# A new stored order and engine choice for the 4,008 steps of an attention and gated MLP kernel

## The chip, the cores and the metric

One core of one Trainium2 chip. The metric is device microseconds (us) of one execution, the median of three runs. PE is TensorE, DVE VectorE, ACT ScalarE, POOL GpSimd, SP the queue that issues the transfers.

## The reference

Eight batches, eight heads, 576 positions, 64 columns a head. Attention has a bias that depends on the two positions through a small MLP; its output goes through a gated block.

```python
scores = scale * np.matmul(q, k.transpose(0, 1, 3, 2))
x = (psi_rel / psi_i)[..., None]
bias = np.maximum(x @ w1 + b1, 0.0) @ w2
scores = scores + bias.transpose(2, 0, 1)[None, :, :, :]
attn = softmax(scores)
x = (attn @ v).transpose(0, 2, 1, 3).reshape(B, S, H * D)
gate = sigmoid(causal_conv_5_taps(x, conv_w))
out = (gate * (x @ w_val)) @ w_out
```

## The kernel before

The program is first written as a list of steps. `Plan.add` takes for each step the engines that may do it, with a booked duration for each in us, a function that issues it, and the steps that it depends on. Nothing is issued then. `Plan.order` reads a stored table, `ORDER`: two bytes for each of the 4,008 steps, which give the step's number and which of its engines does it. The steps are issued in that order, so each engine's queue is the table's order cut to that engine, and buffers are handed out in the table's order as well. The booked durations and due times are not read when the kernel is built; the table was found with them elsewhere.

```python
for lo, hi in zip(code[:n], code[n:]):
    t = self.tasks[(lo + 256 * hi) // 4]
    t.on, t.done = t.engines[lo % 4], True
```

The stages are these.

The bias: 36 groups of 16 rows (`bias_rows`). Four `relu` steps of a group write the hidden values: the first on ACT (L329), the others on DVE or POOL (L331). `bias_mm` multiplies on PE (L350). `bias_fin` evicts on ACT (L369) or DVE (L371). `bias_store` writes to DRAM and `load_bias` reads skewed rows back.

The weights: `weight` decodes eight blocks of 64-bit numbers on DVE with six `double_step` steps each (L432 to L456), and splits each into two f16 parts (`w_hi`, `w_sub`, `w_lo`). All six steps are booked alike:

```python
[("V", 0.38 * n / 512 + 0.05)]
```

Attention: 32 steps of `pair`, each for two heads of a batch and four or five blocks of 128 queries. For each block PE multiplies (`qkm` L712, `qkr` L728), DVE adds the bias and finds the maximum (`logits` L758), ACT takes the exponential (`expo` L770). In 24 of the pairs the result is split in two f16 parts: `top` copies (L209 on ACT, L211 on DVE, L213 on POOL), `rest` and `rest8` subtract (L232 on DVE or POOL, 1,024 and 128 columns), and `swap` transposes by a transfer (L935). In eight pairs `norm` scales (L820 on POOL, L227 on ACT) and `tp` transposes on PE (L901). `piece` (L970) multiplies by the values, `vlo` (L667) being the low part of these.

The gated block (`mlp`), one for each batch: the convolution (`taps` L1163), `split_hi` and `split_lo` (L220 on DVE), `val` (L1231), the gate (`gf` L1241), `ghi` (L209, L211 or L213) and `glo` (L232), then `outp` (L1297), `ote` and the store. `ghi` and `glo` of the wider part issue two instructions, of 256 and of 64 columns. Between two `qkm` of a pair the table places steps of other pairs and of the gated blocks.

Of the kernel before, what the change touches and what calls it, by code (L numbers as in the profile page):

```python
# [51 lines left out]
    'w*booAkxY-'
    'XeN2%FTPAD?#qA>@nus`XLJ%c67gHvWr#5?maB@w@MVh2Ym)oPEB!{!e*z7nR3OBv2c9+H6l3cFHrMklLFStCNR@>L}_6MC>+8+p38mY|}cSe7o$tH98ZtoAnL@4P?O&b~whS%WYWvaDoemp6q#Yi-'
    'kXg6{-_YX43(@wTouPD_*FPHy?RK+TG4@oidz}6pnOC#UdUvp0AuFF3Num`-'
    'yJ*{{hfney>psn5rHHWQmJL=bbuTT`qRZ(i<f$%7zlxmoL+#;@IrTl3{wmpeEG~HUTSI0?PM0v+yciJ3SBMSG?#668fL$MEV!V`(cmG60d{lpKP$#9CI)1hiuRP32tzEJnO0>x6y&IH+yn{H<-'
    'Ta2`$-ht#uM5D1uwEDwZy*&K3oNA<}nbDY=#*=(i5Ph!ZN3E9vqjoUs_XKm*dNUO6bn~5r*Eb#vC#hbs)$PAK?e#O+DK;A8lW9Ri<Vel?7zXzZZuCDb=VOg_pc5=4Xre+EsbZ-Vs?-`8I-'
    '9G15$AA%q-'
    'dtg?3DASNirNM^fk>2UTrBh{=fJi327|SuoA=AU^KQnvYEsr?sSQ(k}S8WPHtbaISR=ib(OqEPG@@kQkl*&fuOy}@q^*$PlCh=whMv`$zkIo=ZntYimqnMW^Z@u4lmzrxZSj~Y4>@et<tEFdok8?d*'
    'Gz}uO);2VZK~^Gw${<DaT}*c#UOwu^oB$uQ@n(sTv6TJpH`i8tiAFO1C!7Mri+_pz-'
    '?3{@$<xmvuV%GCanLWT~2C;3lEy2CJ!Y3?}pOj}ijgUf|{!UQ}$&q~LJcU8!^@bDnJlf>`9ESH5cG3V0Nkrm3_P3YT+k4-'  # L60
    'xg{<%E)q#cg(nE0b8wbn{OrAzI2hH)EBmyHw_gpV$1gdZTA57Gt$iDx1#bo2_Ig60i6Al}dXQFSMJjPCL=X`_;xc-fWfp0SiIH1q>$6`-'
    'AMTnqfN0R4>;b42z>lI@=|SW2)!Ok<@gW@BC2X8IIWebX3q_99%7zcRbM-'
    'O66|F>#MNky4)D2CW_5%ceGtx8vjt=CEFGrgOX#<?|V<J6U;l+;I^7D{M^?k?2i6ZW+*y+ZdMp^BAM~Hsj=igmSlfG42Iw$_ydzE9*u<qK`C-'
    ';Q#2S+BnKlZPSb3H6NAol=4m!3J%$xjl95nk$P1}yGy#u7!Z92r!{chKmX<Y>@46_vyWSZ2YV2D))AT5u&HnY9@La?*DZ=0B_TE;!fw6|f7(Cr_IbP4Ou{V`!jiR|MJTK1XSH+UGO4NCwEw?1uUMSP'
    'WQaP2V#FLd;Sow>7!&YmyewucO)oFc@^ZM#RpC4mjBeFaG%0()9{AGW@A9(Y*$V<`Kw?bh@BpL{YBTiR59t?TI?<7O9Ml_Lbw&LwhERjj}+%G3nzHG{=abb8dPQ<+3KAEiitXiwnWp^r9alx|ERKCD'
    'uvZZ>Xna<??xmQd$^ZnvrSnU>4#dN*Ve!n+#Hwvv%CRFKoYVF^BHi74>U+PS2@Jb3tvakh|yXE*lCYXIs+1q<{Fu>RmJ{l+c;|~eA8k9sAYITNXxm=1DL|LjRnXHp96ec;2ce!oEq*2sx)5mtKlWw}'
    ')okru8rlUFfWm&2C{2tg{@#+{Vb?~0|4+E^*Yfh$UZ&q663i+DN9%<WNcYHXkcSrpJzerG_55payM-rmc>yL*1vEY;cICx0c2F}3HHy%FcmjmNz)b6MSnF&0LEa!A#SP-'
    '`Lsh9DEj)k!C@0=;kcQqP!gp0=L1Wxz^n`!$fS8oL~<WKVss9mU24ZM+xCy5+G!>hAMGFUpB<MMo?*;1rD`*xLLGcR!-UiL)gnBs^hgo{UQo88$-'
    'rc*X&+v|JI@0v^{Z>(hRmMc}e`<2YgzNE|VdovVxIhD@D6O!<^o&X<gcf3hQ&>bjx!fYfO_H}#xfj^ke#57pwlW-'
    '&^WFt{A_F6ocionGb<B8C3>xp=w_@i_(Q%ZNrl}xEz%VrmH^`TTLSG*m$HwyP7)o5}+Wk37ZW~<xk4RT#vp_$>A1Z^$a?4{wj|Ge{YVOkhZMq|xXgOL;5?jQ(~aj_Kp*zIvn+CjoCbFLik<rG^g6is'  # L70
    'C9j>iRzFOpO)Uo61`*Q4vwG*&8~@01%JZ#WYF`L8PNYSYJd$aj+dK)Ld;PNmZHfU9*it>1qx!#+|Axp<)|W36UJ`Jmq$j{2j#*s|@|+XI3eGsEWw3j#5L_25o;-#-'
    '7s7<PL5WH_3RCmpF$m1MS9a@6WilouP*LPJASIDN=7!Elr1I&F=hV7$%V5i1PK6-'
    '8^w_JRxVw%U<sg1{UvyTd#gWravgjKeEC(HkZE#!w92eq&869Bn>~BwJ!^GT0oqJ3scOGqlT%O>rWgNJ@bq$?z;Eh&H<s&O7L1rIe@YkZYXi9|FPa^riSbQ%}E@RRo*#K!FX~?FwWZj$kfigJ-efaX'
    'UTVX@;DxmNy)RyMb=UqOot|9j`Bxc|8=*y3-k-J)6tsB5~3mpc2u1aGKK;ghH{_Xa@4w4@D)FF8)(1lMPGBR2%l8au4nk?=Q=P4{p<bZdh-'
    '0d)<Ec{Yc+79FOb{c=ttP?*3qczvuCP=;ZU>c%tw(fj5W=SuCY%)99og8Zx6yBR16(OZCAJ_K##L8>&{rzpIriqwz%ZRx6Q=Co=Hr%XNE?|A0l~C43ldwac0T!;Z#NY_mq0KK`WA>!%K4>3TN#-'
    'iY9^%77@45o$s+oOf*bB0CWt6J%kX^-'
    'pufJc*~q9bTAL8=ASzK(j^AVmmI$QbMuY9E{WDcAmSuKDfhJ*wK?IjN?mgs!PKbRd_ce{|bKUSiCY$N!1DF3&O*&N)<XZ(_w48#~)y11zvWnfKN3ZtBBqRgfmD|%>$elTy84V>XvD?D@tNG!dM4SYn'
    '5uRe=ZHj952Z(TCok?URkM)xHKm#Ba6f4d@f`c5*a=f6g`sNk<Mgu6IU|q{yI{?dzxe_lYz&;;|+=Eg4P<6Pmt4?pIFRNb)^|3H+?yK3qE3g+QoVdlV>w_+jjzeS^2_+lMb8R^HOo{6{67${X7^?yz'
    'u3p+S#vQyDvq*n{7Eeoe1$>Bv<&l+k@SZ`eT0(%YV;C=5bnIDB2y)a>eze_{B@5K{Q`();=ozrt)E{3qQyApAJWiV?1g1t2O5!{n4k>p2n5?V|4%5@iaVBM1ypzZ_3#4@SW)|20!6O<Kb6RKDY>XX!'
# [1318 lines left out]
```

## Time and profile before

| what | value |
|---|---|
| median of 3 runs | 670.96 us (669.21 to 675.23) |
| span of the profiled execution | 671.1 us; nothing outside the span is recorded |
| mean granted TensorE clock | 0.991 |
| PE busy | 639.2 us (95%) |
| DVE, ACT, POOL busy | 606.8, 571.7, 484.8 us |

The span runs from the first to the last instruction. The busy time of an engine is the time in which at least one of its instructions ran. What is missing from 671.1 us on PE, 31.9 us, is the time in which PE had nothing to do.

### The profile page before, as it was taken

The page shows a single profiled execution, that of the slowest core. Times are in us where ns is not written, and L with a number is a line of the kernel's source. Part 1 is how long each engine was busy: PE and PEld are TensorE (multiplying, and loading weights), DVE is VectorE, ACT ScalarE, POOL GpSimd, SP SyncE. Part 2 cuts the span into 40 slices and gives each one's busy share as a digit, 9 for nine tenths or more (in the row PEclk, how much of TensorE's full clock was granted, in tenths as well). Part 3 has the DMA queues.
Part 4 walks back from the last instruction along what each step waited for, and adds up shares of the span by engine and source line. Part 5 has one row for each costly group of instructions (what it writes and reads, how often), then busy time and mean ns, then how long its engine had stood idle before and what let it go on. Part 6 is the DMA issues. An engine that isn't in the chain of part 4 may idle for free. (4 is left out here: it accounts for less than half of the span.)

```text
span 671.1 us, 17133 instructions
## 1 busy us (share of the span) xinstructions
PE 639.2 (95%) x6176; PEld 408.4 (61%) x6176; DVE 606.8 (90%) x1609; ACT 571.7 (85%) x1262; POOL 484.8 (72%) x540
## 2 busy tenths in 40 slices
...
GB/s 177 262 300 310 317 213 208 100 111 173 175 211 206 204 223 195 234 207 198 213 209 177 193 217 184 214 187 171 199 225 95 167 201 196 230 183 164 115 79 95
DMA packets 279109, 129.80 MB, mean 193 GB/s; under 512 B 255600, under 2 KB 255856, under 8 KB 279024
## 3 DMA queue, kind: packets, MB, share of 16 engines
...
## 5 line engine op out<-in xcount | busy, mean ns | idle before, releaser
L232 POOL TENSOR_TENSOR t_d<-t_d 128x1024 f16<-128x1024 f32 (+1 forms) x180 | 243.7, 1370 | 56.6 <-ACT t_d L209 33.6
L770 ACT ACTIVATE t_d<-t_d,nm 128x576 f32<-128x576 f32 x288 | 221.5, 771 | 32.7 <-DVE nm L758 31.2
L758 DVE CUSTOM_DVE_ANT_0 t_d<-t_sp,bias 128x576 f32<-128x576 f32 x256 | 186.8, 751 | 21.1 <-PE t_sp L712 14.4
L712 PE MATMUL t_sp<-t_qk 64*128 64x288 f32 x1024 | 172.7, 432 | 7.1 <-DVE nm L758 6.8
L712 PEld LDWEIGHTS t_sp<-t_qk 64*128 64x128 f32 x1024 | 96.9, 186 | 56.3 <-DVE nm L758 20.3
L970 PE MATMUL t_ps<-t_pt,t_w 128*64 128x256 f16 (+1 forms) x1664 | 125.2, 300 | 5.3 <-DVE t_xp L1026 2.2
L209 ACT CAST t_d<-t_d 128x576 f16<-128x576 f32 x156 | 100.5, 667 | 10.5 <-DMA t_pt<-t_d 4.3
L1231 PEld LDWEIGHTS <-wv 128*128 128x128 f16 x768 | 72.4, 98 | 31.8 <-issue 12.6
L970 PEld LDWEIGHTS <-t_w 128*64 128x64 f16 x1344 | 71.4, 112 | 24.4 <-issue 16.6
L1231 PE MATMUL t_ps<-xh,wv 128*128 128x256 f16 (+1 forms) x480 | 68.2, 286 | 0.1
L1163 DVE SCALAR_TENSOR_TENSOR t_ps<-t_xp,convw,t_ps 128x288 f32<-128x288 f32 x126 | 64.7, 517 | 2.2 <-ACT t_ps L1154 0.9
L1297 PE MATMUL t_ps<-wo,gh 128*128 128x512 f16 x240 | 58.1, 380 | 0.0
L770 ACT ACTIVATION_READ_ACCUMULATOR t_d<-t_d,nm 128x1 f32 x288 | 54.9, 191 | 0.0
L350 PE MATMUL t_ps<-rel,w 128*32 128x288 f32 (+17 forms) x352 | 48.9, 501 | 4.8 <-DVE rel L331 2.1
L331 POOL TENSOR_SCALAR rel<-gt,sct,nb 128x432 f32<-128x432 f32 (+10 forms) x14 | 32.9, 2355 | 21.7 <-PE t_ps L350 21.3
L820 POOL TENSOR_SCALAR t_d<-t_d,rinv 128x576 f32<-128x576 f32 x57 | 42.5, 759 | 8.2 <-DVE rinv L800 4.2
L213 POOL TENSOR_SCALAR t_d<-t_d 128x576 f16<-128x576 f32 x47 | 35.7, 764 | 15.7 <-ACT t_d L770 8.2
L331 DVE TENSOR_SCALAR rel<-gt,sct,nb 128x576 f32<-128x576 f32 (+17 forms) x94 | 46.3, 553 | 0.1
L901 PE MATMUL t_ps<-ident,t_d 128*128 128x128 f32 x324 | 43.3, 278 | 1.9 <-POOL t_d L820 0.8
L901 PEld LDWEIGHTS t_ps<-ident,t_d 128*128 128x128 f32 x324 | 35.3, 140 | 14.0 <-issue 5.1
L1128 POOL TENSOR_TENSOR t_w<-t_w 128x576 f32<-128x576 f32 x19 | 27.5, 1448 | 17.8 <-DVE t_w L1128 13.6
L1231 PE MATMUL t_ps<-xl,wv 128*128 128x256 f16 (+1 forms) x240 | 38.5, 285 | 0.6 <-DVE xl L220 0.6
...
## 6 DMA issues: line engine op xcount, KB each, us to landing
...
```

Of the source, the lines that this page charges most:

```text
L209: A.copy(out=out, in_=in_)
L232: (V if e == "V" else G).tensor_tensor(out=out, in0=in0, in1=in1, op=ALU.subtract)
L331: (G if e == "G" else V).tensor_scalar(out=rel[g].t[:, 0:w], in0=src, scalar1=sct[:, mm : mm + 1], scalar2=nb1, op0=ALU.mult, op1=ALU.max,)
L350: T.matmul(pb[32 * g : 32 * g + 32, 0 : y - x], lhsT=w28, rhs=rel[g].t[:, x:y], start=True, stop=True, tile_position=(0, 32 * g),)
L712: T.matmul(ts[a][:, j, 0:hw], lhsT=qk.t[r, c * P : (c + 1) * P], rhs=qk.t[r, x : x + hw], start=True, stop=True,)
L758: V.tensor_tensor_reduce(out=part(c, a).rearrange("p (j f) -> p j f", j=2), in0=sp.t[:, :, 0 : S // 2], in1=bias.rearrange("p (j f) -> p j ...
L770: A.activation(out=part(c, a), in_=part(c, a), func=AF.Exp, bias=nms[c][:, a : a + 1], scale=-1.0, accum_out=sums[c][:, a, 0:1],)
L901: T.transpose(t[:, k * P : (k + 1) * P], es[c].t[:, (k0 + k) * P : (k0 + k + 1) * P], ident)
L970: T.matmul(po.t[r, 0:256], lhsT=vt.t[:, v, r], rhs=pt[:, x, :, :] if tr else pt[:, :, x, :], start=(t == 0 and m == 0), stop=(t == 4 and m ...
L1163: V.scalar_tensor_tensor(out=o, in0=x, scalar=wt, in1=t, op0=ALU.mult, op1=ALU.add)
L1231: T.matmul(pm.t[:, 0:w], lhsT=weights["wv"][wi][:, k, d * P : (d + 1) * P], rhs=xb.t[xi][:, k, 0:w], start=(q == 0 and k == 0), stop=(q == ...
L1297: T.matmul(pm.t, lhsT=gb.t[gi][:, k, o : o + P] if o < 256 else gx.t[gi][:, k, :], rhs=weights["wo"][wi][:, k, :], start=(q == 0 and k == ...
```

## The change

The table is replaced by another one. Nothing else that is issued differs: the steps, their functions, dependencies, buffers and booked durations are the same. `plan.at` and `t.at` are labels that nothing reads when the kernel is built. The change says of the new table that it was searched with random landings of the transfers and random phases of the TensorE clock, and with the dearer decoding steps booked.

```diff
 ORDER = (
-    'c-l=@4`?cPo;UA}W|EA_B#y}>nIvPJBx5orlVp-iUgkaQ;etKvVZnl3>|qc0uwaWl+`}IBa2FTs;exwZaKQx&zQbKyu#0c8i(Oo>hdu1#9o}KVF7|L2A6T%53-++beShQYa^Ly=`F=m&&-'
...
 class Plan:
     def __init__(self, bufs):
-        self.tasks, self.bufs, self.kind = [], bufs, ""
+        self.tasks, self.bufs, self.at = [], bufs, ()
...
         t = Task(engines, fn, [d for d in deps if d is not None], takes)
+        t.at = self.at
...
+        plan.at = ("bias", m)
...
-        plan.kind = "_t" if tr else ""
+        plan.at = ("pair", n)
```

Decoded, the two tables compare as follows. PE does the same 1,031 steps, 417 of them at the same place of its order; the PE work that stands ahead of a step differs by 0.4 us in the median of all steps and by under 3.8 us for 95 of 100. Pairs and gated blocks follow each other as before. 386 of the 4,008 steps have another engine. In all, DVE has 1,287 steps for 1,284, ACT 950 for 951, POOL 468 for 470. The moves, as steps that leave and that come:

| step | DVE | ACT | POOL |
|---|---|---|---|
| relu of the bias | 12 leave, 4 come | | 4 leave, 12 come |
| bias_fin | 13 leave, 3 come | 3 leave, 13 come | |
| top | 10 leave, 19 come | 44 leave, 28 come | 26 leave, 33 come |
| rest | 6 leave, 7 come | | 7 leave, 6 come |
| rest8 | 15 leave, 24 come | | 24 leave, 15 come |
| ghi | 5 leave, 10 come | 16 leave, 18 come | 16 leave, 9 come |
| glo | 14 leave, 15 come | | 15 leave, 14 come |

The net moves by stretch of the table: up to the first `logits` steps of pair 9, the relu and bias_fin moves above and few others; from there to those of pair 14, DVE gains four glo, three rest and two top and loses two acc; from there to those of pair 24, DVE gains eight rest8 and four top and loses two ghi; after that, DVE gains seven ghi, four norm and two top and loses four glo and two rest. Of single steps, a glo of the third batch's second part goes from DVE to POOL, and a ghi of the fifth batch's first part from DVE to ACT. The first loads of weights and values stand in another order on SP, the later ones nearly in the old one.

## Rows read from the trace of the kernel before

**Rows 1.** Busy time of each engine by stretch, granted clock, DMA share, GB/s.
```profile
core 0: us, PE busy (x) PEld busy (x) DVE busy (x) ACT busy (x) POOL busy (x), PEclk, DMA share, GB/s
0.00:25.00 25.00, 18.44 (x134) 6.50 (x134) 20.38 (x54) 18.18 (x35) 7.29 (x18) 1.00 0.64 209
25.00:50.00 25.00, 23.05 (x155) 7.12 (x152) 25.00 (x60) 22.92 (x48) 19.28 (x9) 1.00 0.90 284
50.00:75.00 25.00, 22.16 (x181) 11.21 (x178) 24.80 (x68) 22.82 (x51) 14.97 (x17) 1.00 0.96 306
75.00:150.00 75.00, 75.00 (x650) 52.05 (x650) 72.53 (x220) 71.65 (x181) 53.65 (x76) 1.00 0.54 181
150.00:200.00 50.00, 43.67 (x478) 30.00 (x475) 49.36 (x129) 47.65 (x107) 39.60 (x40) 1.00 0.93 185
200.00:325.00 125.00, 123.03 (x1271) 82.19 (x1269) 110.92 (x296) 113.93 (x246) 103.18 (x113) 1.00 1.10 207
325.00:475.00 150.00, 141.77 (x1424) 91.41 (x1422) 136.63 (x353) 122.53 (x271) 119.33 (x123) 0.97 1.01 196
475.00:650.00 175.00, 174.88 (x1811) 119.19 (x1810) 159.09 (x419) 148.69 (x322) 124.54 (x147) 1.00 0.85 171
```

**Rows 2.** Groups of instructions, 0 to 75 us: busy, mean ns, idle before, releaser.
```profile
L331 DVE TENSOR_SCALAR rel<-gt,sct,nb 128x576 f32<-128x576 f32 (+17 forms) x94 | 46.3, 553 | 0.1
L331 POOL TENSOR_SCALAR rel<-gt,sct,nb 128x432 f32<-128x432 f32 (+10 forms) x14 | 32.9, 2355 | 21.7 <-PE t_ps L350 21.3 <-DVE rel L331 0.2
L369 ACT ACTIVATE t_be<-t_ps,cadd 128x288 f32<-128x288 f32 (+52 forms) x61 | 27.9, 505 | 6.1 <-PE t_ps L350 3.2 <-DVE t_be L371 2.5 <-DMA bias_d<-t_be 0.2
L350 PEld LDWEIGHTS t_ps<-rel,w 128*32 128x32 f32 x352 | 15.3, 113 | 36.9 <-DVE rel L331 21.2 <-ACT t_be L369 5.1 <-DVE t_be L371 3.4
L371 DVE TENSOR_SCALAR t_be<-t_ps,cadd 128x288 f32<-128x288 f32 (+18 forms) x19 | 7.3, 396 | 0.0
```

**Rows 3.** Timeline of the bias stage, DVE and POOL: start, us, instruction.
```profile
13.86 3.25 DVE L331 TENSOR_SCALAR rel<-gt,sct,nb 128x512 f32<-128x512 f32 x6
14.23 2.64 POOL L331 TENSOR_SCALAR rel<-gt,sct,nb 128x432 f32<-128x432 f32 x1 [5.93 <-PE t_ps L350]
18.47 5.81 DVE L331 TENSOR_SCALAR rel<-gt,sct,nb 128x416 f32<-128x416 f32 x14
```

**Rows 4.** Busy time by stretch around the two falls of the clock.
```profile
345.00:350.00 5.00, 3.38 (x51) 1.83 (x51) 4.97 (x9) 1.84 (x6) 2.85 (x3) 0.89 1.09 207
350.00:355.00 5.00, 5.00 (x40) 2.87 (x34) 3.33 (x15) 2.68 (x7) 4.25 (x7) 0.50 0.42 98
...
457.00:460.00 3.00, 1.70 (x8) 0.58 (x6) 2.96 (x4) 2.49 (x5) 2.49 (x2) 1.00 0.87 201
460.00:465.00 5.00, 4.48 (x26) 2.88 (x28) 5.00 (x15) 2.68 (x5) 2.73 (x3) 0.66 0.64 105
```

**Rows 5.** Timeline, ahead of the same two places: POOL and DVE.
```profile
345.37 2.56 POOL L232 TENSOR_TENSOR t_d<-t_d 128x1024 f16<-128x1024 f32 x2
345.48 2.14 DVE L232 TENSOR_TENSOR gxl<-t_w,gxh 128x64 f16<-128x64 f32 x1
...
457.51 2.13 POOL L232 TENSOR_TENSOR t_d<-t_d 128x1024 f16<-128x1024 f32 x1 [1.40 <-ACT t_d L209]
457.56 2.23 DVE L211 CAST gh<-t_w 128x256 f16<-128x256 f32 x1
```

**Rows 6.** Timeline, two more such places.
```profile
358.32 2.72 DVE L667 SCALAR_TENSOR_TENSOR t_w<-t_w,vsc 128x640 f16<-128x640 f32 x1
...
395.52 4.08 DVE L220 SCALAR_TENSOR_TENSOR xl<-t_xp,bsc,xh 128x640 f16<-128x640 f32 x2
```

**Rows 7.** Groups of instructions, DVE, by shape: rest and ghi.
```profile
L232 DVE TENSOR_TENSOR t_d<-t_d 128x1024 f16<-128x1024 f32 x17 | 23.0, 1352 | 0.5 <-ACT t_d L209 0.2
L211 DVE CAST gh<-t_w 128x256 f16<-128x256 f32 x9 | 4.9, 555 | 0.1
```

**Rows 8.** Waits view: DVE for the transposing transfers; total us, times, longest.
```profile
DVE t_d L758 <- DMA t_pt<-t_d: 3.0, 4, 1.2
```

**Rows 9.** Groups of instructions, DVE: one of the six decoding steps.
```profile
L448 DVE SCALAR_TENSOR_TENSOR t_w<-t_d,t_w 128x512 int32<-128x512 int32 (+1 forms) x9 | 6.1, 677 | 0.1
```

More of the change, by code (lines that the diff above doesn't have):

```diff
@@ L52 @@
[L52 to L79, printed above, removed]
@@ L107 @@
[L107 to L110 removed]
+    'c-nnee`qpynm6w|nn~VCGKpg{CX-~6Ow5=}l1Va2Cds@nzJ~?(uwV}t+`}&Ra1RT%*u^gPuwV~&v4;h_*u{doxZn%+a2I#+U2Jg=yV%163wE)GdsuM6E_ShpJ>0_{zQ;Y^F>n98XJ(!spXc*D&)0Eg9C6WAuhtS2NoY9Qi@7~DhL^XbM$;F(Z?XGxp}@zj$5x-i){Zm^`DnZuE7{7gyxK~n?G9(MQ^~k`ZGUJu=;Nv0$o7{`'
@@ new lines @@
+    '-#+L%dd^Xw)nMhYa~yU@G_gfjoS>2kg6;~{tUEXM@Y1iClrYE_MUN)OrZX7k<*;a=B=?l^a8StemcAf9E{!VZGG2}u$Rt76>Pls7VKg-^@kzYdY}AJ>7H?at5}9hHJGP8(j->p-=P0_GwQ@}_*7damp>Sv9w7Y`iz)PWZhK}^YY|PDnDGr80yfJD$k>oCybwq2Ph(>8UER@&!akAM+xSg%fzLWC!bF4S*%j65ie2Fh-0*^X>'
+    '6mpW?$?+$lLZv8|t$5{r)YhfKZ@mA|-4kNTKB?j3u0%?bJtWN}ux>CLt=iMoIhtJ;#NqdRfdTt+oD-92$t+`nf=6SSlr<bw2%9Aou{;uURzfqfOLa17D{v&mj490Fw777ayKem@P1spE=xo$9$!5D)l^rFe)p-_odEDMwx5rgVysy!08J}B^#}aM-4^o{$9~);<GoQy3LLi;>Xx<ak`En&T3`LUJ)NjJgLb}zd#iR9+RFW&@'
+    'Otq|xoux`9TOlbIV^w<IelG9!c<m0Kt1uY){DCTM>9XzJoRjyvZ6A!r;h<3bLVO`m`>26?^O0aZ)GYM<1K;ouk2PfpzA%h956Ko1mp@U8)>8D%u%>FOSgeYzhS@DPDiR%yLjgSGm~&QxbUW<!L|t#Z|HJS``QKP?ES?BkB4sh0R8pC8ryI!T@`ZZPXSc@Ek^FNZtKV6%hl{<w?e|TW`>oNFYAuoo4~Dg<N8m&UoMW$?;p3_L'
@@ new lines @@
+    'x63}if6#C>tJ!?3lWQkp9(TR<tH8K77`8{_&O0g1aFj`7#8?yT*Sc&MYvANA*26=2uiuvq<UWnWh+-*KDo`ylO;bVo%ip${^-QIf#R-z4N8DCE&J=P*4PL5-qT6pL`7W>2Ed+KLN|it92$7!EW{*13F;bM8G9~qgad|M3Gp#mbu_ZLVLEoQLa@oAKQ{V>O;*jU~RGRJyL|-_S<Od&GNNd$zZv>jHw#6pe?GAU)Su@l-p68x%'
+    'HNu%f&gt?-==h7zW%G%m)A@=&%GlhZ$IJ4r;hVnia)R^@+YF3+o>cI)R?t80PG!BlX4}>6^#`G0#r;!H&Wri5PTyY)d^H^9X^b2*RPfiOnR2D&&4e|zP&mwL@H!odRyl@`v7D^L`2;T53JhhjTOEQg*-D)d{!pSJee`wu`F72daV7&laFOA~R3w_o70WSMv4}CNjfkhRLOM4tbtHSb;OJJ01!pCn^@hChM6%?At1#lPRBQD{'
+    '$Cxj4BZJ3V*&J7E)f>$y-tDzwQG!nOqOty<Nisuoy>XI;YopiC_xqp4Go^gGofu@2+2JT#qU@uwD>vvAhYmMIGh+=l))3oqd{}L=qc$wZYU2v-9N{dsYRxu9a&@=I%#TWr;Rs9gJBwY93u{UiE93Rq{DLTzd#&;B+fF>Gu~!K8kIw#+z!!ZXwMZRyM=rQee0EM8c!uBc_T>DyufYq&q=qLhN(0{&n@Wcx_c<~1M11Iv#)dt|'
```

64 lines of the change are left out of this document (28 added, 36 removed).

## The prediction

> **What bounds the kernel now.** I read the table of stretches first, since the change touches the whole program. PE has work for nearly all of the time, so the most that an order can win is what PE stands idle or runs at half clock [rows 1]. From 75 to 150 us PE is busy for 75.00 of 75, and from 475 to 650 for 174.88 of 175: nothing is to be had there. Three stretches have room. In the first 75 us PE lacks 11.35 (25.00 less 18.44, 23.05 and 22.16); from 150 to 200 it lacks 6.33; from 325 to 475 it lacks 8.23, and the granted clock there is 0.97 in the mean, so some 0.03 x 150 = 4.5 us more are lost to the clock.
>
> Next I asked in each stretch who is late. From 25 to 75 us DVE is busy for 49.80 of 50 and ACT for 45.74, POOL only for 34.25 [rows 1]. The groups of that stretch say the same from the other side: PE's weight loads for the bias wait 21.2 us for DVE's relus [rows 2]. So DVE sets the pace there. From 150 to 200 us DVE is again full (49.36 of 50).
>
> In the middle no engine is full. There I looked for the places where the clock falls. It stands at 0.50 from 350 to 355 us, which is the lower level (1.2 of 2.4 GHz) for the whole row, and at 0.66 from 460 to 465; each fall comes right behind PE having had little to do (3.38 of 5.00, 1.70 of 3.00) [rows 4]. Just ahead of both a small DVE step lasts over 2 us: a subtraction of 64 columns 2.14, a cast of 256 columns 2.23, and each begins within 0.11 us of a POOL subtraction of 1,024 columns and ends with it [rows 5]. The mean of that cast is 0.56, this one included [rows 7]. DVE stood behind POOL, the next `logits` came late, PE ran dry, and then its clock fell. Two more such places cost DVE as much without a fall of the clock [rows 6].
>
> Transfers are not on the path: DVE's waits for the transposing transfers are 3.0 us in the whole run, 1.2 at most [rows 8].
>
> **The change, stretch by stretch.** Nothing is added or removed; the price of a move is what one engine loses and another gains, and it counts where that engine is late.
>
> First 75 us. DVE loses eight relus net at 46.3 / 94 = 0.49 us, that is 3.9, and ten bias_fin at 7.3 / 19 = 0.38, that is 3.8: together 7.7 us [rows 2]. POOL gains 8 x 2.36 = 18.8 us and has 75 - 41.5 = 33.5 free [rows 1, 2]. ACT gains 10 x 27.9 / 61 = 4.6 us [rows 2]; it is idle for 4.26 us from 25 to 75 and for 6.82 before that, much of which lies ahead of the first work [rows 1]. Against the 7.7 stands what a POOL relu does to DVE: six DVE relus of up to 512 columns that ran beside one took 0.54 each, fourteen without one, of 416 columns and near, 0.42 [rows 3]; at 0.42 us for 416 columns the 96 more explain at most 0.10 of the 0.12, so one POOL relu costs six of DVE between 0.1 and 0.7, and eight more cost 1 to 6; I take 3. DVE is ahead by 4.7. The ends are 0, if ACT becomes the late engine, and -4.7; I take half, -2.4, because ACT's remaining idle time is about what it gains.
>
> What a text of the chip would make of the same move: the Trainium skill, SBUF — State Buffer, section "SBUF: two separate sides", says that the port pair which DVE and GpSimd share is locked for a whole instruction, whoever has it first, and that the other then fully blocks. By that, each POOL relu could stop a DVE relu for up to its own 2.36 us and the eight would cost 18.8, not 3. The rows of the relus do not show it; those of the subtractions do [rows 3, 5]. I go by the rows for each kind of step.
>
> 75 to 200 us. PE is full to 150, so the gain of the first stretch is carried through. From 150 DVE is the late one, and of its 4.7 us 2.3 are left over. Other moves are few here. Ends 0 and -2.3; DVE was idle for 0.64 us of 50, ACT for 2.35 [rows 1], so DVE is nearest to the bound and I take two thirds, -1.6. That the decoding steps are dearer than booked is true: one of the two dear steps takes 0.68 us in the mean where 0.43 is booked [rows 9]. But the decoding stays where it was, in the same engine and nearly the same place, so this cannot give more than what DVE is relieved of.
>
> 200 to 325 us. DVE gets some work back: three `rest` at 1.35 are 4.1 us [rows 7], and four small `glo` come with them. It was idle for 14.08 of 125 [rows 1], which covers that; without this cover it would cost the 4.1 and more. I take 0, from -2.0 (all of PE's idle time) to +3.
>
> 325 to 475 us. The first fall of the clock costs 1.62 us of idle PE and (1 - 0.50) x 5 + (1 - 0.89) x 5 = 3.0 of clock, 4.7 in all; the second 1.30 and 0.52 of idle PE and (1 - 0.66) x 5 = 1.7, 3.5 in all [rows 4]. Together 8.2. The new table has the very `glo` off DVE that began the first, and the `ghi` that began the second. On the other hand the kinds of DVE step that can stand behind POOL (rest, rest8, top, ghi, glo, split_lo, vlo) are 134 before and 160 after; four of 134 stood for about 1.8 us or more, two of these with a fall of the clock [rows 4 to 6]. At that rate 160 give 4.8, and the cost is 8.2 x 160 / 134 = 9.8: a loss of 1.6 in place of a gain of 8.2. Nothing in the trace of before says which meetings the new order brings. I take the middle, -3.3; the ends are -12.7 (8.23 + 4.5) and +5 (one more place of the dearer kind).
>
> 475 us to the end. PE has nothing to gain. DVE gets seven ghi (0.56 each with their waits, 3.9) and gives up two `rest` (2.7) [rows 7], the other moves nearly cancel; it has 15.9 us of 175 free [rows 1]. I take +1.0, from 0 to +5. The order of the last 24 us, `val` and `outp` of the last batch, is nearly the same.
>
> The sum: -2.4 - 1.6 + 0 - 3.3 + 1.0 = -6.3. The profiled execution has a span of 671.1 and shows nothing around it; the median of the runs is 670.96, the same. 671.1 - 6.3 = 664.8 us.
>
> **The rivals.** *It all lands elsewhere.* ACT takes DVE's place in the first stretch (0 for -2.4), and the meetings of DVE and POOL come at the old rate (+1.6). For it: ACT is nearly full from 25 to 200 us. Against it: PE's weight loads wait four times longer for DVE's relus than for ACT's evictions (21.2 to 5.1 us) [rows 2]. 671.1 - 1.6 + 1.6 + 1.0 = 672. In this case the random landings were beside the point, as the waits for transfers are small: the change would not do what it says. *Slower: DVE behind POOL.* The 26 more DVE steps of that kind meet POOL, and each meeting ahead of a `logits` costs an average of the two, 4.1 us. With three more than before: 671.1 - 4.0 + 3 x 4.1 = 679.4. It decides from three such places on, since two (8.2) less the first two terms (4.0) are within 1%. For it: POOL gets some 19 us more work. Against it: four places in 671 us are few, and two known ones are gone. *Slower: the relus stop DVE too.* 671.1 - 7.7 + 18.8 = 682.2; the fourteen DVE relus in a row and the six beside POOL speak against it [rows 3]. That is where the sentence of the State Buffer page leads. *Much faster.* DVE's relief counts in full (-4.7), PE's idle time from 200 to 325 goes (-2.0) and both falls of the clock go (-8.2): 671.1 - 14.9 = 656.2.
>
> **How the numbers follow.** A measurement of this kernel tells about 1% from no change, 664.3 and 677.7 being the limits. The forecast, 664.8 with 659 to 669, has 0.50, half on each side of 664.3. The first rival, 669 to 675, has 0.22; the slower ones 0.11 and 0.02; the much faster one, 650 to 659, 0.15. Faster by over 1%: 0.25 + 0.15 = 0.40. Slower: 0.13 and 0.01 from the upper end of the first rival, 0.14. Within: 0.46. The range is 655 to 678: it leaves out a third of the much faster case and most of the slower ones, under 0.2.
>
> **What would show it.** In the bias stage: 22 POOL relus, 86 of DVE, DVE's share still near full, the last L350 some 2 us earlier; if instead ACT's share goes over 47.5 of 50 with DVE below, the first rival holds. From 150 to 200 us: PE's 43.67 rises by one to two us. From 325 to 475: no row at 0.50, or other rows at it; the steps of 64 to 256 columns on DVE that last 2 us tell which. If such steps are more than six, and PE's clock falls in more than two places, I am wrong upwards. If PE's idle time is under 20 us in all, I am wrong downwards.

## The result, and the profile after

| | before | after |
|---|---|---|
| median | 670.12 us (20 runs, 664.93 to 675.23) | 676.10 us (20 runs, 670.49 to 683.59) |
| ratio, 95% interval | | 1.0093 (1.0063 to 1.0122) |
| span of the profiled execution | 671.1 us | 681.8 us |

The new table is slower by 0.9%, some 6 us; the forecast was 6 us faster. Medians here and below are of all runs, while a ratio leaves out those over 1.5% above the fastest of their kernel, so that the quotient of two medians can differ from it. The profiled execution of the changed kernel is the longest of its 20, so I also use a second trace of the same kernel (after_again, span 676.5 us), and say of each reading whether both show it. Line numbers after are 27 to 31 lower than before: L301 is the relu on DVE and POOL, L339 and L341 bias_fin, L320 the bias multiplication, L685 `qkm`, L731 `logits`, L941 `piece`.

The stretch table of the changed kernel (columns as in [rows 1]):

```profile
0.00:25.00 25.00, 18.47 (x142) 6.14 (x142) 20.07 (x45) 19.94 (x39) 18.19 (x23) 1.00 0.74 247
25.00:50.00 25.00, 20.13 (x144) 6.09 (x140) 23.72 (x53) 23.89 (x53) 18.34 (x11) 1.00 0.88 283
50.00:75.00 25.00, 21.98 (x180) 10.80 (x180) 24.83 (x62) 22.75 (x51) 21.08 (x18) 1.00 0.89 285
75.00:150.00 75.00, 75.00 (x644) 51.02 (x645) 71.39 (x220) 71.75 (x179) 52.45 (x74) 1.00 0.51 176
150.00:200.00 50.00, 42.61 (x387) 28.67 (x388) 44.47 (x113) 40.97 (x92) 37.74 (x36) 0.90 0.85 167
200.00:325.00 125.00, 120.66 (x1237) 80.74 (x1236) 113.08 (x304) 108.08 (x239) 88.84 (x96) 0.99 1.01 196
325.00:475.00 150.00, 143.57 (x1493) 93.78 (x1485) 134.16 (x361) 124.76 (x274) 118.59 (x127) 0.95 1.03 202
475.00:650.00 175.00, 173.06 (x1807) 116.41 (x1806) 160.09 (x431) 142.72 (x324) 128.01 (x144) 1.00 0.87 177
```

Beside [rows 1], three things stand out. DVE's 49.80 of 50 from 25 to 75 us is 48.55, ACT's 45.74 is 46.64, and PE has not gained. From 150 to 200 us PE is busy for 1.06 us less, and the granted clock is 0.90 where it was 1.00: 5.0 us of clock (0.10 x 50). From 325 to 475 the clock is 0.95 where it was 0.97 (0.99 in after_again).

The groups of the first 75 us, for [rows 2]:

```profile
L301 DVE TENSOR_SCALAR rel<-gt,sct,nb 128x576 f32<-128x576 f32 (+17 forms) x86 | 48.5, 619 | 1.2 <-PE t_ps L320 1.2
L301 POOL TENSOR_SCALAR rel<-gt,sct,nb 128x416 f32<-128x416 f32 (+13 forms) x22 | 47.1, 2150 | 9.0 <-PE t_ps L320 8.7 <-DVE rel L301 0.3
L339 ACT ACTIVATE t_be<-t_ps,cadd 128x272 f32<-128x272 f32 (+31 forms) x71 | 31.2, 507 | 3.3 <-PE t_ps L320 3.2
L320 PEld LDWEIGHTS t_ps<-rel,w 128*32 128x32 f32 x352 | 13.8, 111 | 39.4 <-DVE rel L301 18.5 <-ACT t_be L339 8.6 <-ACT rel L299 6.3
L341 DVE TENSOR_SCALAR t_be<-t_ps,cadd 128x15 f32<-128x15 f32 (+8 forms) x9 | 3.5, 396 | 0.0
```

DVE does 8 relus fewer and is busy with relus for longer: 48.5 us in place of 46.3. PE's weight loads wait less for DVE (18.5 for 21.2) and more for ACT's bias_fin (8.6 for 5.1).

From 170 to 195 us the stretches of the changed kernel, and of the kernel before ahead of them from 165 to 190:

```profile
165.00:170.00 5.00, 2.75 (x21) 1.46 (x18) 4.90 (x15) 3.43 (x8) 2.27 (x1) 1.00 1.05 188
175.00:180.00 5.00, 3.51 (x22) 2.12 (x21) 4.82 (x15) 4.97 (x10) 4.28 (x6) 1.00 0.92 194
180.00:185.00 5.00, 3.50 (x46) 2.65 (x46) 5.00 (x11) 5.00 (x11) 5.00 (x6) 1.00 1.13 173
185.00:190.00 5.00, 4.86 (x53) 3.37 (x47) 5.00 (x14) 5.00 (x13) 5.00 (x4) 1.00 0.91 247
```
```profile
170.00:175.00 5.00, 2.83 (x15) 1.77 (x17) 4.16 (x13) 5.00 (x11) 4.10 (x3) 0.83 1.00 229
175.00:180.00 5.00, 4.04 (x19) 2.06 (x18) 3.77 (x10) 5.00 (x13) 4.49 (x9) 0.82 0.93 176
185.00:190.00 5.00, 3.61 (x16) 2.18 (x18) 5.00 (x12) 4.27 (x9) 4.58 (x4) 0.70 1.05 210
190.00:195.00 5.00, 5.00 (x72) 4.22 (x69) 3.37 (x9) 4.60 (x11) 4.29 (x5) 0.62 0.62 118
```

PE has about as little to do in both, yet only after the change does the clock drop to the lower of its two levels, 1.2 GHz, for part of four rows. What PE waits for there, from its timeline in the changed kernel (the bracket has the idle time ahead and what ended it):

```profile
165.33 0.52 PE L941 MATMUL t_ps<-t_pt,t_w 128*64 128x256 f16 x6 [1.43 <-DMA t_pt<-t_d]
173.75 0.66 PE L507 MATMUL t_ps<-ident,wsc 128*128 128x128 f32 x2 [1.71 <-DVE wsc L502]
186.39 2.96 PE L685 MATMUL t_sp<-t_qk 64*128 64x288 f32 x8 [2.56 <-DVE nm L731]
```

First a transposing transfer comes late, then DVE's row of weight maxima, then a `logits`, behind which PE runs at half clock. after_again has the same three waits, of 1.67, 1.71 and 1.75 us.

The waits view, the changed kernel first, then the kernel before, for the transposing transfers ([rows 8] has DVE's of before):

```profile
ACT t_d L178 <- DMA t_pt<-t_d: 6.9, 6, 2.4
PE t_ps L941 <- DMA t_pt<-t_d: 6.1, 6, 1.8
DVE t_d L731 <- DMA t_pt<-t_d: 5.3, 4, 1.8
```
```profile
ACT t_d L209 <- DMA t_pt<-t_d: 4.3, 7, 0.9
PE t_ps L970 <- DMA t_pt<-t_d: 1.0, 1, 1.0
```

### The profile page after: what moved, and what is told of

The parts are those of the page before. It is cut to its first block, busy times and chain, and to the rows that moved or that the text cites. A ratio compares the mean times of both kernels' runs of the same rounds, so it can differ in the third digit from the quotient of the medians.

```text
span 681.8 us, 17176 instructions
## 1 busy us (share of the span) xinstructions
PE 643.3 (94%) x6176; PEld 410.1 (60%) x6176; DVE 609.5 (89%) x1612; ACT 565.6 (83%) x1259; POOL 493.2 (72%) x536
## 4 chain that ended last, share of the span: by engine, by line
PE 64%; DVE 10%; DMA 8%; ACT 5%; POOL 3%; issue 2%; DVEq 0%; ACTq 0%; POOLq 0%
PE t_sp L685 17%; PE t_ps L941 12%; PE t_ps L1202 12%; PE t_ps L1268 10%; DMA t_pt<-t_d 8%; PE t_ps L874 5%; DVE t_d L731 3%; PE t_ps L987 3%; ACT t_d L743 3%; PE t_sp L701 2%; POOL t_d L201 2%; PE t_ps L1011 2%; ACT t_d L178 1%; DVE rel L301 1%; DVE t_ps L1134 1%
## 5 line engine op out<-in xcount | busy, mean ns | idle before, releaser
L201 POOL TENSOR_TENSOR t_d<-t_d 128x1024 f16<-128x1024 f32 (+1 forms) x170 | 238.5, 1419 | 73.5 <-ACT t_d L178 55.0
L731 DVE CUSTOM_DVE_ANT_0 t_d<-t_sp,bias 128x576 f32<-128x576 f32 x256 | 186.4, 750 | 26.5 <-PE t_sp L685 15.9
L685 PE MATMUL t_sp<-t_qk 64*128 64x288 f32 x1024 | 175.8, 439 | 8.3 <-DVE nm L731 7.7
L941 PE MATMUL t_ps<-t_pt,t_w 128*64 128x256 f16 (+1 forms) x1664 | 127.8, 300 | 8.6 <-DMA t_pt<-t_d 6.1
L685 PEld LDWEIGHTS t_sp<-t_qk 64*128 64x128 f32 x1024 | 98.8, 190 | 59.6 <-DVE nm L731 22.6
L178 ACT CAST t_d<-t_d 128x576 f16<-128x576 f32 x140 | 90.4, 663 | 9.2 <-DMA t_pt<-t_d 6.9
L1202 PEld LDWEIGHTS <-wv 128*128 128x128 f16 x768 | 73.2, 99 | 33.9 <-issue 13.1
L941 PEld LDWEIGHTS <-t_w 128*64 128x64 f16 x1344 | 71.8, 112 | 26.9 <-issue 21.0
L1202 PE MATMUL t_ps<-xh,wv 128*128 128x256 f16 (+1 forms) x480 | 70.6, 290 | 0.6 <-DVE vsc L623 0.6
L182 POOL TENSOR_SCALAR t_d<-t_d 128x576 f16<-128x576 f32 x54 | 41.0, 761 | 19.2 <-ACT t_d L743 7.5
L320 PE MATMUL t_ps<-rel,w 128*32 128x288 f32 (+17 forms) x352 | 46.5, 491 | 8.7 <-ACT t_be L339 3.3
L301 POOL TENSOR_SCALAR rel<-gt,sct,nb 128x416 f32<-128x416 f32 (+13 forms) x22 | 47.1, 2150 | 9.0 <-PE t_ps L320 8.7
L301 DVE TENSOR_SCALAR rel<-gt,sct,nb 128x576 f32<-128x576 f32 (+17 forms) x86 | 48.5, 619 | 1.2 <-PE t_ps L320 1.2
L196 ACT ACTIVATE t_xp<-t_ps,vsc 128x256 f32<-128x256 f32 (+1 forms) x72 | 29.5, 412 | 16.7 <-PE t_ps L987 6.5
L178 ACT COPY t_pt<-t_ps 128x512 f32<-128x512 f32 (+1 forms) x82 | 36.7, 498 | 3.5 <-PE t_ps L874 3.2
```

Of the source, the lines that this page charges most:

```text
L178: A.copy(out=out, in_=in_)
L201: (V if e == "V" else G).tensor_tensor(out=out, in0=in0, in1=in1, op=ALU.subtract)
L301: (G if e == "G" else V).tensor_scalar(out=rel[g].t[:, 0:w], in0=src, scalar1=sct[:, mm : mm + 1], scalar2=nb1, op0=ALU.mult, op1=ALU.max,)
L320: T.matmul(pb[32 * g : 32 * g + 32, 0 : y - x], lhsT=w28, rhs=rel[g].t[:, x:y], start=True, stop=True, tile_position=(0, 32 * g),)
L685: T.matmul(ts[a][:, j, 0:hw], lhsT=qk.t[r, c * P : (c + 1) * P], rhs=qk.t[r, x : x + hw], start=True, stop=True,)
L731: V.tensor_tensor_reduce(out=part(c, a).rearrange("p (j f) -> p j f", j=2), in0=sp.t[:, :, 0 : S // 2], in1=bias.rearrange("p (j f) -> p j ...
```

## The experiments

A time that the clock took is worked out for one execution as (1 - its mean granted clock) x its span; of several it is the mean. "Step (9, 1)" is `qkm` of pair 9, block 1, the second score step of that pair, and so on; where the expectations of after_again and after_wod speak of the first score step of pair 9, their numbers are those of (9, 1). Where a step stands was found by matching PE's instructions with the decoded table.

**Halves, and order against engines.** The new table as a list of (step, engine), cut at a step of PE; "rest" is what is left, in the order of the table named:

```diff
-ORDER = new
+ORDER = new[up to (9, 1)] + old[rest]             # new_to_200
+ORDER = old[up to (9, 1)] + new[rest]             # new_from_200
+ORDER = old order, engines of new                 # eng_only
+ORDER = new order, engines of old                 # ord_only
```

new_to_200. 

> The new table up to the second qkm step of pair 9 (about 200 us), the old one for all later steps. Theory A (the loss is made between 150 and 200 us, where the trace of the changed kernel falls back by 6 to 8 us while neither DVE nor ACT is full): the whole loss is here, ratio to the kernel before 1.008 to 1.011. Rival B (the loss is spread over the table, as DVE stands behind POOL in more places): a third of it, 1.002 to 1.005.

new_from_200. 

> The old table up to the same step, the new one for all later steps. Theory A: no loss or a small gain, 0.995 to 1.001, since in the one trace the later part loses 4 us from 200 to 270 and wins and loses 6 us after that. Rival B: 1.004 to 1.008.

eng_only. 

> The old order with the new choice of engines for all steps. If the loss comes from what the engines have to do (more steps of DVE that share its path with POOL, ACT fuller in the bias stage), it is all here, 1.007 to 1.012. If it comes from the order, 0.997 to 1.003.

ord_only. 

> The new order with the old choice of engines. The mirror: 0.998 to 1.002 if the engines make the loss, 1.007 to 1.012 if the order does. If both this and the old order with the new engines lose, order and engines belong together and either table is fitted to itself.

Measured: new_to_200 677.39 us, ratio 1.0124 (1.0076 to 1.0171); new_from_200 675.20, 1.0101 (1.0053 to 1.0148); eng_only 730.54, 1.0921 (1.0881 to 1.0962); ord_only 736.51, 1.0993 (1.0941 to 1.1045). Order and engines of a table belong together, as the last sentence of ord_only's expectation has it: the order of one table with the engines of the other costs 9 to 10%. So most of the later runs cut the table across time.

Both halves of the time cost something, and both more than either theory gave them. Alone they add to 2.25%, with some 0.7 either way; the whole costs 0.93%. The halves add to more than the whole by more than the errors.

**One stretch alone.**

```diff
-ORDER = old
+ORDER = new[up to (7, 2)] + old[rest]                         # new_to_150
+ORDER = old[up to (7, 2)] + new[up to (9, 1)] + old[rest]     # new_150_200
+ORDER = new[up to (7, 2)] + old[up to (9, 1)] + new[rest]     # old_150_200
+ORDER = old[up to (9, 1)] + new[up to (14, 1)] + old[rest]    # new_200_300
+ORDER = old[up to (14, 1)] + new[up to (24, 0)] + old[rest]   # new_mid
+ORDER = old[up to (24, 0)] + new[rest]                        # new_tail
```

new_to_150. 

> The new table up to the third score step of pair 7 (150 us), the old one from there. The traces of the parts so far give this stretch no gain and no loss (that step lies at 153 to 154 us with either table, PE full from 75 to 150). Theory additive (each stretch costs by itself; 150 to 200 us 0.38%, 300 to 484 nothing, 484 to the end 0.32%): ratio 0.998 to 1.003. Rival front (the new first 150 us leave the engines in a state that costs later, which would explain 1.24% for the first half alone): ratio 1.005 to 1.010.

new_150_200. 

> The old table, with only its part from the third score step of pair 7 to the second of pair 9 (about 150 to 200 us) ordered and placed as in the new one. Theory A (the loss of the first half sits between 160 and 195 us, as late transfers and the falls of the clock that they bring): ratio to the kernel before 1.006 to 1.012, PE's lag from 155 to 190 us of its own work grows by about 15 us instead of 9. Theory B (the loss comes from what the new first 150 us leave behind, engines that are late by then): ratio within 0.997 to 1.003, and the clock keeps 1.00 from 150 to 200 us.

old_150_200. 

> The new table, with only its part from the third score step of pair 7 to the second of pair 9 taken from the old one. Theory A: most of the loss of the first half is gone and that of the second half stays; since the halves did not add up before (1.012 and 1.010 alone, 1.009 together), ratio 0.998 to 1.005. Theory B: the loss stays, ratio 1.007 to 1.012.

new_200_300. 

> The old table, with only its part from the second score step of pair 9 (about 202 us) to the second of pair 14 (300 us) as in the new one. Forecast for this stretch 0, from -2.0 to +3 us. Theory additive: what is left of the 0.93% after the other parts (0.93 - 0.38 + 0.05 - 0.32 = 0.28% for this stretch and the first 150 us together), ratio 0.999 to 1.004. Rival: all that remains lies here and the parts add to more than the whole, ratio over 1.005.

new_mid. 

> The old table, with only its part from the second score step of pair 14 (300 us) to the first of pair 24 (484 us) as in the new one: the stretch where the forecast put -3.3 us, because the new table breaks the two meetings of DVE and POOL that stand ahead of the falls of the clock at 348.9 and 461.5 us. If that term holds, ratio 0.993 to 0.997 and no 5 us row under 0.70 from 325 to 475 us. Rival, from the traces so far (the same steps lie 189 us apart in the mean with either table): new meetings and falls come in their place, ratio 0.998 to 1.003.

new_tail. 

> The old table up to the first score step of pair 24 (484 us), the new one from there. Forecast for this stretch +1.0 us: ratio 1.000 to 1.003. Theory from the traces so far (from that step to the end the new table takes about 190 us, the old one about 188): +2 to +3 us, ratio 1.003 to 1.005. Rival: all of the 1.0% that the second half cost alone lies here, ratio 1.008 to 1.011.

| new part | time | ratio, 95% interval | forecast of the stretch | measured |
|---|---|---|---|---|
| to 150 us | 672.39 | 1.0048 (1.0013 to 1.0083) | -2.4 (0 to 75 us) | +3.2 us |
| 150 to 200 | 672.72 | 1.0038 (1.0004 to 1.0071) | -1.6 (75 to 200 us) | +2.6 |
| 200 to 300 | 670.05 | 1.0015 (0.9984 to 1.0045) | 0 | +1.0 |
| 300 to 484 | 671.06 | 0.9995 (0.9957 to 1.0034) | -3.3 | -0.3 |
| 484 to the end | 672.86 | 1.0032 (1.0000 to 1.0065) | +1.0 | +2.2 |
| all but 150 to 200 | 675.76 | 1.0020 (0.9982 to 1.0057) | | +1.3 |

(Measured: the ratio less 1, times 671.) The five parts add to 1.28%, each with some 0.35 either way, so about 0.8 on the sum; the whole is 0.93%, and 1.18% (1.0057 to 1.0179) in after_again. By the ratios the parts make the whole within their errors. By what the time consists of they don't. The next table splits the mean time over all runs into what the clock took and the remainder, each less that of before in the same call (95% intervals from the spread of the runs):

| new part | clock, us | remainder, us |
|---|---|---|
| to 150 us | +0.3 (1.6 either way) | +3.3 (0.9) |
| 150 to 200 | -0.3 (1.7) | +2.2 (1.4) |
| 200 to 300 | -1.3 (1.4) | +2.1 (0.8) |
| 300 to 484 | +0.1 (2.7) | +0.5 (1.1) |
| 484 to the end | +1.0 (2.2) | +2.8 (1.2) |
| to 200 (new_to_200) | +3.7 (2.1) | +4.8 (1.6) |
| from 200 (new_from_200) | +4.3 (3.2) | +1.8 (1.3) |
| all (after_again) | +3.8 (2.8) | +4.4 (1.7) |

The five parts add to 10.9 us of the remainder with 2.4 either way, and the whole has 4.4 with 1.7: that does not add up. For the clock they add to -0.2 with 4.4 either way against 3.8 with 2.8, which is too wide to tell. A rival to "each stretch costs by itself" was not tested: a mixed table has one or two seams, where queues and buffers of one table meet those of the other, and no run prices a seam alone. So what a part costs and what its seams cost can't be told apart. None of the five parts alone shows the clock's 4 us. What stands is that the middle costs nothing that shows.

old_150_200 decides little between its theories. Its ratio of 1.0020 lies in theory A's range, but the mean of all its runs is 4.5 us above that of before (2.8 either way), and its trace has a row of 0.50 from 170 to 175 us, among the old steps.

In new_to_150 PE comes to step (7, 2) at 151.2 us, 0.9 later than before. This holds without a seam: over the eight traces that have the first 150 us of the new table unchanged (7, 2) is at 150.7 to 152.5 us, over the eight with those of the old one at 149.9 to 150.7, so 1.2 earlier in the mean. The trace of new_to_150 then reaches (9, 1) at 204.9 us, against 202.3 before, behind a row of 0.50 from 180 to 185 us, where only the old table was at work. Ahead of that fall PE's waits of over 0.5 us are 1.69, 0.73, 0.60, 0.67 and 0.59 us; before_again has the same five, of 1.50, 0.55, 0.60, 0.68 and 0.59, with a clock of 1.00. In old_150_200 (9, 1) is at 208.8. I counted over all traces that leave the steps from 150 to 200 us as in one of the tables: with the old table both there and ahead of it, rows under 0.90 between 160 and 195 us are found in 1 of 6 (new_mid; not in the two of before, new_from_200, new_tail and new_200_300); with the new one in either place, in 8 of 9. (9, 1) then comes at 204.9 to 209.9 us; with the old table and no such rows it comes at 201.9 to 202.6. new_150_200 falls between its two theories (1.0038), with rows of 0.89 and 0.50 from 170 to 180 us, and new_to_150 between its two (1.0048), so in time both the new stretch and what stands ahead of it have a share, seams included. A share of either alone in the clock is not shown: each count is of single traces, and over the runs the clock took 3.8 us in new_to_150 and 5.2 in new_150_200, against 3.5 and 5.6 for before in the same calls. In new_mid the rival holds, in new_200_300 and new_tail the theory.

**Relus and bias_fin.**

```diff
 # the new table; order unchanged
-16 relus on their new engines
+16 relus on their old engines (8 more on DVE, 8 fewer on POOL)    # after_relu
-13 bias_fin on ACT
+13 bias_fin on DVE                                                # after_fin
```

after_relu. 

> The new table, with the 16 relus that changed between DVE and POOL back on their old engines (8 more on DVE, 8 fewer on POOL). Theory contention (POOL's 22 relus slow those of DVE: their mean was 553 ns before and is 619 now): the mean falls to 540 to 575 ns, DVE's sum in relus stays at 47 to 51 us although it has 8 more, and the first score step of pair 2 comes within 1 us of 84.3. Rival (DVE's relus are slower for another reason): the mean stays over 600 ns, the sum goes over 52 us and the step comes over 2 us later.

after_fin. 

> The new table, with the 13 bias_fin that went from DVE to ACT on DVE again (some 13 x 0.39 = 5 us more for DVE, 6 less for ACT). Theory both (in the first 75 us DVE and ACT are now both at their limit): the first score step of pair 2, at 84.3 us in the changed kernel, comes 1 to 4 us later. Rival ACT (ACT alone took DVE's place, DVE has room): it comes 1 to 3 us earlier and PE's waits for ACT's t_be fall from 8.6 us to under 6.

Each of these two ran once (674.55 and 677.30 us), for its trace alone. after_relu, groups of the first 75 us:

```profile
L300 DVE TENSOR_SCALAR rel<-gt,sct,nb 128x496 f32<-128x496 f32 (+17 forms) x94 | 46.7, 557 | 1.3 <-PE t_ps L319 1.2
L300 POOL TENSOR_SCALAR rel<-gt,sct,nb 128x432 f32<-128x432 f32 (+10 forms) x14 | 31.8, 2273 | 22.0 <-PE t_ps L319 21.2 <-DVE rel L300 0.6
L319 PEld LDWEIGHTS t_ps<-rel,w 128*32 128x32 f32 x352 | 14.1, 115 | 38.2 <-DVE rel L300 12.6 <-ACT t_be L338 10.5 <-ACT rel L298 7.6
```

With 8 relus more DVE is busy with relus for 1.8 us less, and step (2, 0) comes at 83.8 us, against 84.3. Theory contention holds, with a sum just under its range (46.7, forecast 47 to 51): at 46.7 / 94 = 0.497 us the 86 relus of the changed kernel would take 42.7 us; they take 48.5, at nearly the same width (436 and 438 columns in the mean). The eight relus that went to POOL cost DVE 5.8 us, 0.7 each, more than they took off it (8 x 0.497 = 4.0). That DVE is relieved brings PE next to nothing: the weight loads wait 12.6 us for it in place of 18.5, but 10.5 in place of 8.6 for ACT's bias_fin, and the traces with an unchanged first 75 us of the new table have (2, 0) at 83.7 to 85.4 us.

after_fin, PE's weight loads in the same view:

```profile
L319 PEld LDWEIGHTS t_ps<-rel,w 128*32 128x32 f32 x352 | 14.4, 112 | 41.6 <-DVE rel L300 22.5 <-ACT rel L298 5.7 <-ACT t_be L338 5.3
```

The wait for ACT falls to 5.3 us, that for DVE rises to 22.5, and (2, 0) comes at 88.2 us, 3.9 later. Theory both holds, though one sign of its rival came too (the wait for ACT under 6 us): DVE has no room for what ACT took from it, and by after_relu ACT is as late as DVE. One thing was unexpected. From 150 to 200 us after_fin has the new steps in the new order and keeps a clock of 1.00: from (7, 0) to (9, 1) it takes 58.3 us, as before (58.5), where the changed kernel takes 64.4. Here the transposing transfer that PE waited for in the changed kernel lands sooner. The view of transfers, the changed kernel from 157.9 us, then after_fin from 161.8 us (last number: us to landing):

```profile
t_pt<-t_d SPq DMA_TRANSPOSE x1, 7.3
```
```profile
t_pt<-t_d SPq DMA_TRANSPOSE x1, 5.6
```

In six traces with the new order there (the changed kernel's two, after_sp, after_relu, new_to_200, new_150_200) PE waits 1.0 to 1.9 us for this transfer and the clock falls; in after_fin neither happens.

**The late transfer.**

```diff
 # the new table; SP's queue
-swap(7, 1), ldv 10, qk_ld 8, swap(7, 2), ldv 9, swap(7, 4), swap(7, 3), swap(6, 0), ...
+swap(7, 1), qk_ld 8, swap(7, 2), swap(7, 4), swap(7, 3), swap(6, 0), ldv 9, ... swap(6, 2), ldv 10   # after_sp
-swap(7, 0), w_ld wo 3, swap(7, 1)
+w_ld wo 3, swap(7, 0), swap(7, 1)                      # after_wod; before_wod: the same on the old table
```

after_sp. 

> The new table, with two entries of SyncE's queue moved: the loads ldv of pairs 9 and 10 stand again behind the transposing transfers swap of pair 6, as in the old table. If these loads, issued ahead of the transposing transfers, make the latter late, ACT's and PE's waits for them from 157 to 170 us (2.41 and 1.43 us) go down by over 1 us each, and the time falls by 2 to 5 us: ratio 1.002 to 1.007. If the transfers are late for other reasons, nothing changes: 1.008 to 1.011.

after_wod. 

> The new table with one entry moved: the last load of weights (wo, 512 KB), which SyncE issues 0.47 us ahead of the transposing transfer swap of pair 7, chunk 1, goes ahead of the one before it (swap of chunk 0). In the traces so far that transfer lands after 5.4 to 5.6 or after 7.2 to 7.8 us. Theory landing (beside the load it lands late, PE waits 1.4 to 1.9 us for it, then the clock falls between 170 and 195 us): it lands within 6 us, PE does not wait for it, no row under 0.80 from 165 to 195 us, the first score step of pair 9 at 202 to 204 us in place of 208.7, ratio 1.002 to 1.007. Rival (the falls have other reasons): the rows under 0.80 stay, ratio 1.007 to 1.012.

before_wod. 

> The old table with the same entry moved. The old order took a landing of 7.2 to 7.4 us without a fall of the clock in three traces of four, and one of 5.4 to 5.6 with one in two of three; theory landing thus expects little here, ratio 0.995 to 1.002; the price of moving the load ahead of swap of chunk 0, if that one lands later by it, ratio 1.002 to 1.006.

after_sp: 675.60 us, ratio 1.0067 (1.0033 to 1.0100); PE waits 1.59 us for the transfer and ACT 2.58, as in the two traces of the changed kernel (1.43 and 1.67, 2.41 and 2.65). The ratio is at the upper end of the theory's range and its interval takes in both ranges, so the waits decide: the loads behind the transfer are not what makes it late. after_wod: 683.44, 1.0227 (1.0185 to 1.0268); before_wod: 676.41, 1.0139 (1.0100 to 1.0177). The transfer now lands within 5.0 and 4.7 us, but the load waits on SP and holds swap(7, 0) behind it (issued at 156.5 in place of 152.2 us, 154.8 in place of 151.5), and PE stands for 4.05 and 4.66 us in one piece; after_wod still has a row of 0.50, from 165 to 170 us. Both lose by the price put down for before_wod alone, over twice its upper end. So whether the late landing brings the falls in the changed kernel stays open; against it speaks that the old order takes a landing of 7.2 to 7.3 us with a clock of 1.00 in four traces.

**The clock alone.** Work for PE in its three waits of 1.43, 1.71 and 2.56 us:

```diff
+WARM = {(5, 1, 4): 7, "wg": 9, (7, 1, 4): 14}
...
             def piece(e, g, t, po):
...
+                for _ in range(WARM.get((n, g, t), 0)):
+                    T.transpose(po.t[:, 256 : 256 + P], ident, ident)
...
     def wg_mm(e):
         t = bank(wt_)
+        for _ in range(WARM["wg"]):
+            T.transpose(t[:, 2 * P : 3 * P], ident, ident)
```

after_warm. 

> The new table with added work for PE alone, transposes of the identity into columns of a PSUM bank that nobody reads: 7 behind the last piece of pair 5 (ahead of the wait of 1.43 us), 9 at wg_mm (1.71 us), 14 behind the last piece of pair 7 (2.56 us). The waits stay, PE is only kept at work in them. Theory clock (the falls of the clock at 173 and 187 us, 5 us by the rows, are what the stretch costs): no row under 0.95 from 170 to 195 us, time 3 to 5 us less, ratio 1.001 to 1.006. Rival (the waits cost it, the clock goes with them and PE is waited for by nobody then): ratio 1.008 to 1.012; above 1.012 if the added work delays what stands behind it.

```profile
170.00:175.00 5.00, 4.44 (x30) 3.04 (x30) 4.32 (x15) 5.00 (x11) 4.10 (x4) 1.00 1.02 216
175.00:180.00 5.00, 4.15 (x41) 2.76 (x40) 5.00 (x15) 5.00 (x13) 4.41 (x8) 1.00 0.98 181
185.00:190.00 5.00, 4.78 (x83) 3.67 (x78) 5.00 (x12) 4.69 (x12) 5.00 (x6) 1.00 0.90 144
190.00:195.00 5.00, 4.45 (x38) 3.32 (x34) 5.00 (x11) 3.81 (x9) 5.00 (x4) 1.00 1.09 162
```

In its trace the clock keeps 1.00 and (9, 1) comes at 203.6 us, 5.1 earlier than in the changed kernel. The time does not follow: 675.45 us (12 runs), ratio 1.0082 (1.0050 to 1.0113). Over the runs the clock took 3.7 us in place of 7.7, and the remainder of the mean time rose from 668.7 to 671.8. The half of theory clock that speaks of the rows is right, the half that speaks of the time is not. An estimate of why: the added transposes take 2.7 and 1.2 us, 3.9 in all, and in an execution without falls the waits are shorter (after_fin: none, 0.98 and 0.76 us), so about 2 us stick out. That was not shown.

**Second traces.**

after_again. 

> The changed kernel once more, on the chip of the two others and with another trace. Theory chance (from 160 to 195 us a fall of the clock comes in some executions of either table, in five of six traces with the new one there and in one of four with the old): whether this trace has rows under 0.80 from 165 to 195 us is open, about five in six; the first score step of pair 9 then comes at 207 to 209 us, without such rows at 202 to 203. Ratio 1.007 to 1.012.

before_again. 

> The kernel before once more, for a second trace. In its first trace the engines wait 9.8 us in all for the transposing transfers, the least of all traces so far (9.8 to 33.9). Theory chance: this trace shows over 12 us. Rival (the old table has the shorter waits): under 12 us.

after_again: 678.83 us, 1.0118 (1.0057 to 1.0179), rows of 0.61, 0.71 and 0.68 from 175 to 195 us, (9, 1) at 209.9. In that call the mean time is 8.2 us above that of before (677.4 to 669.2); the clock took 7.3 and 3.5 us, so 3.8 of the 8.2 are clock and 4.4 are not. before_again: span 665.5 us, clock 1.00, and the engines wait 20.2 us for the transposing transfers, where the first trace of the same kernel has 9.8. Of the eighteen traces without those of eng_only and ord_only, that first one has the shortest such waits; the others have 14.9 to 33.9, with either table.

## Why the prediction was wrong, by its own steps

**First 75 us, -2.4: failed, and this is the first step that did.** Two terms of it were off. The price of POOL's relus was taken as 3 us, from 1 to 6; it is 5.8. So DVE's 7.7 us on paper became 46.3 + 7.3 - 48.5 - 3.5 = 1.6 us. And the 4.6 us more of ACT were taken to fit into its idle time; they do not: PE's weight loads wait 8.6 us for ACT's bias_fin in place of 5.1, and 10.5 where DVE is relieved (after_relu). PE's last bias multiplication begins at 65.0 us in place of 63.7, step (2, 0) is at 84.3 in place of 84.0, and (7, 2) comes 1.2 us later in the mean of eight traces with either table. So what came lies a little beyond the end "0, if ACT becomes the late engine", and the first rival was nearest here; its sign, ACT over 47.5 of 50, was set too sharp (46.64), since DVE stayed late as well. The Trainium skill, SBUF — State Buffer, section "SBUF: two separate sides", as weighed in the prediction, would have DVE stopped for POOL's whole instruction, by an estimate up to 8 x 2.15 = 17.2 us. The runs show 5.8, and the longest DVE relu of the changed kernel lasted 1.03 us. The truth lay between the two readings, and nearer to the rows.

**75 to 200 us, -1.6: failed.** It carried on the gain that was not there, and "DVE is the late one" did not hold: DVE is busy for 44.47 of 50 us in place of 49.36 (46.73 in after_again), and PE's three long waits there end with a transfer, a small DVE step and a `logits`. What the stretch costs is 1.06 us of PE and 5.0 of clock in the profiled execution; by the ratios 2.6 us for the new steps alone and 3.2 for the new first 150 us, seams included. The sentence "Transfers are not on the path" belongs here: it counted DVE's 3.0 us of the 9.8 that all engines waited, and it rested on one execution, with the shortest such waits of the eighteen traces.

**200 to 325 us, 0: right within its error** (+1.0 measured from 200 to 300; the remainder without the clock rose by 2.1 us, 0.8 either way, which is inside the ends). Whether DVE's free time covered the three `rest` was not tested.

**325 to 475 us, -3.3: failed in size, inside its ends** (-0.3). Both named meetings are gone from the changed kernel, and their falls with them. Of DVE steps that stood behind POOL by over 1.6 us it has three there (a `glo` of 2.16 at 429.2, two `vlo` of 2.58 and 2.76 at 387.0 and 434.3), where it had four. But falls come in other places, and with another cause. The stretches around them:

```profile
350.00:355.00 5.00, 3.24 (x28) 1.87 (x26) 3.24 (x12) 2.61 (x7) 4.85 (x8) 0.93 1.11 223
355.00:360.00 5.00, 5.00 (x19) 2.53 (x15) 2.74 (x8) 3.81 (x10) 3.12 (x4) 0.50 1.09 204
380.00:385.00 5.00, 3.63 (x21) 1.70 (x17) 3.46 (x9) 3.70 (x8) 2.86 (x2) 1.00 1.13 184
385.00:390.00 5.00, 5.00 (x27) 2.85 (x27) 4.04 (x6) 4.13 (x9) 4.63 (x4) 0.50 1.07 222
```

and DVE's timeline just ahead of both:

```profile
352.93 0.76 DVE L731 CUSTOM_DVE_ANT_0 t_d<-t_sp,bias 128x576 f32<-128x576 f32 x1 [1.76 <-DMA t_pt<-t_d]
381.32 0.46 DVE L180 CAST t_d<-t_d 128x576 f16<-128x576 f32 x1 [1.49 <-DMA t_pt<-t_d]
```

DVE stands for a buffer that a transposing transfer still reads; the next `logits` is late, PE runs dry and its clock falls: the chain of the prediction with a transfer in POOL's place. In new_mid, the same steps behind the old table, neither fall is there (no row under 0.90 from 325 to 475 us), and yet nothing is won: before_again keeps 1.00 there with the old table. The 8.2 us that the prediction counted as the price of the old order was the price of that execution.

**475 us to the end, +1.0: right in kind, half in size** (+2.2, in the range to +5).

**The sum.** -6.3 was forecast; the parts measure +8.6, with some 5 either way, the whole +6.2. The rival nearest in its mechanism, "It all lands elsewhere", gave 672 and had ACT right; that the change would "not do what it says" holds, as the waits for transfers did not become shorter. "DVE behind POOL" gave 679.4, nearer to the measured 676.10, but by luck: its mechanism, three more such meetings, did not come. The cause is shown for the first 75 us alone. What stays open: why the clock takes some 4 us more with the whole new table and with either half, while none of the five parts alone shows that, and what the 4.4 us are that are not clock, beyond the 1.2 us that PE is late at (7, 2). None of the runs is clearly faster than the kernel before.
